# Attention's projections of chunk pairs as row tiles, with one PSUM bank per head

## The chip, the cores and the metric

The program runs on one core of one Trainium2 chip. Its time is the device time of one execution in microseconds. Before the change it is 2106.98 us, the median of three runs (2106.40 to 2107.38). The profile is of one more execution, taken by the hardware profiler.

## The reference

The program is a chain of three parts in float32: a linear attention with random features, a mixture of eight experts with balanced gates, and a feed-forward layer. The change touches the first one, for 4 batches, 8 heads, 576 tokens, a head size D of 64 and M = 128 features:

```
def phi(x):                       # x: q or k, scaled by D**-0.25
    proj = einsum('bhsd,md->bhsm', x, omega)
    sq = sum(x * x, -1) / 2
    h = proj - sq
    return exp(h - max(h, -1)) / sqrt(m)
q_p, k_p = phi(q_s), phi(k_s)
kv = einsum('bhsm,bhsd->bhmd', k_p, v)
z = sum(k_p, 2)
num = einsum('bhsm,bhmd->bhsd', q_p, kv)
den = einsum('bhsm,bhm->bhs', q_p, z) + 1e-6
out = num / den
```

## The kernel before, in words

Attention takes about the first 181 us of 2106. It works by units: one unit is a pair of heads of one batch, so there are 16, numbered from 0. The 576 tokens of a unit stand in five chunks (CH), chunk 0 of 128 tokens and chunks 1 to 4 of 112. The two heads of a pair lie in the upper and lower 64 partitions of qk, which holds the transposed and scaled q (index 0) and k (index 1).

What is done for a unit, by the names that the trace shows:

- tr: the transposes of q and k into qk's banks (qkT, L412), which ScalarE scales into qk (L421, L429).
- pr: the projection of a chunk (feat, L432), two products for q and k against bd, the block-diagonal omega: 128 rows of contraction, of which each head's features use 64 and meet zeros in the other 64. Both heads of q and k fill one PSUM bank, 4 x 128 columns.
- mx, nm, nb: VectorE's maximum over the features from that bank (L448), and two small subtractions with the squared norms sq (L450, L452).
- eq, ek: ScalarE's four exponentials of a chunk (exps, L454), which read the bank, with nb as bias; k's come first.
- kv: the sums of features and values over the five chunks, by head; zr and kz are VectorE's scaled copies of them (L484, L490).
- z, jk, den: transposed sums of features, and VectorE's row sums with eq (zT, L496). GpSimd then scales eq by the reciprocal.
- qt: transposes of eq (qpT, L532), copied to qp by ScalarE; nd: the numerators (num, L549), two 64-column tiles of TensorE's array, copied out by ScalarE (xo) and written to DRAM.

A float32 product shows as two records of TensorE in the trace, and a transpose as one.

The order is written out by hand, in rounds: the loop at L622 goes over units i and rounds r = 0 to 4, and PLAN (L612) lists each round's TensorE work and the unit that it belongs to, as an offset. Each round begins with a flush (L373): it issues the round's projection and its reduction, then everything that earlier work had put into later (ScalarE's copies and exponentials) and laterv (VectorE's, by a number), with nm and nb in between. So a chunk's exponentials are issued in the round after its projection. Chunk r is projected in round r. Each engine takes its instructions in the order in which they are issued.

Seven PSUM banks serve all of tr, pr, kv, qt and nd; an eighth is z's. A new name takes a bank that was given up, and its first product waits for the last reader of what was there. The program's own semaphore counts tell which reader that is.

Between the rounds stand steps that prepare the next phase: wprep, the weights (L639, after round 4), and xprep (L641), by XSTEPS after rounds 1 and 3 of units 8 to 15: loads, a ScalarE copy of 128x768 (L259), VectorE subtractions.

Of the kernel before, what the change touches and what calls it, by code (L numbers as in the profile page):

```python
# [9 lines left out]
F32 = mybir.dt.float32  # L10
# [9 lines left out]
def performer_moe_kernel(ctx, tc, q, k, v, omega, wg, w1, w2, win64, wout64, out):  # L20
    nc = tc.nc
# [274 lines left out]
    with ExitStack() as actx, tc.manual_schedule():  # L296
        pp = actx.enter_context(tc.tile_pool(name="pp", bufs=7, space=PSUM))

        def bank(name):
            return pp.tile([P, 512], F32, tag="b", name=name)  # L300
# [70 lines left out]
        later, laterv = [], []  # L371

        def flush(ft=iter(())):  # L373

            todo, todov = list(later), sorted(laterv, key=lambda x: x[0])
            later[:], laterv[:] = [], []
# [55 lines left out]
        def feat(u, c):  # L432

            qk, sq = T["qk", u], T["sq", u]
            o, n = CH[c]
# [5 lines left out]
            mx = a2.tile([P, 4], F32, tag="mx", name=f"mx{u}_{c}", bufs=4)  # L441
            nm = a2.tile([P, 4], F32, tag="nm", name=f"nm{u}_{c}", bufs=4)
            nb = a2.tile([P, 4], F32, tag="nb", name=f"nb{u}_{c}", bufs=4)
            ps4 = ps.rearrange("p (i m) -> p i m", i=4)
            eq = a2.tile([P, 2, M], F32, tag="eq", name=f"eq{u}_{c}", bufs=16)
            ek = a2.tile([P, 2, M], F32, tag="ek", name=f"ek{u}_{c}", bufs=7)
            T["eq", u, c], T["ek", u, c] = eq, ek
            nc.vector.tensor_reduce(mx[:n], ps4[:n], AX.X, ALU.max)  # L448
            yield
            nc.vector.tensor_tensor(nm[:n], sq[:n, c], mx[:n], ALU.subtract)  # L450
            yield
            nc.vector.tensor_tensor(nb[:n], nm[:n], sq[:n, c], ALU.subtract)  # L452

            def exps():  # L454
                for i in (2, 3, 0, 1):
                    dst = (eq, ek)[i // 2][:n, i % 2]
                    nc.scalar.activation(dst, ps4[:n, i], AF.Exp, bias=nb[:n, i : i + 1])

            T["tail feat"] = ps4, eq, ek, nb
            later.insert(0, exps)  # L460
            yield
# [137 lines left out]
        flush(feat(0, 0))  # L599
# [11 lines left out]
        NORM, RED, SPL = (0, 1), (2, 4), 4  # L611
        PLAN = [  # L612
# [625 lines left out]
```

## Time and profile before

| | |
|---|---|
| median of three runs | 2106.98 us |
| the profiled execution | 2107.69 us |
| its span | 2105.9 us |
| TensorE busy in the span | 2091.3 us |
| VectorE | 1784.4 us |
| GpSimd | 1448.0 us |
| ScalarE | 1060.7 us |
| mean granted TensorE clock | 0.999 of full speed |

The span is what the profile shows from the first to the last instruction; the profiled execution took 1.8 us more. Busy times are of the whole span, most of which is the two later parts. What attention waits for is read from its own stretch, 52 to 94 us for its steady middle.

### The profile page before, as it was taken

To read this page: it belongs to the slowest core of one execution; us is meant where nothing else is said; L and a number is where in the kernel's file an instruction comes from. 1 tells how busy PE (TensorE), PEld (TensorE's weight loads), DVE (VectorE), ACT (ScalarE), POOL (GpSimd) and SP (SyncE) were. 2 spreads that over 40 slices of the span, in tenths; PEclk is the share of its full clock that TensorE was granted. 3 is DMA by queue.
4 is the path that set the end of the run, shared out by engine and by line. 5 is a ranking of instruction groups with operands and counts; after the bars stand their busy time and mean duration, and the time that the engine had idled before them with its cause. 6 is when DMAs were issued, how large, how long until landed. Compare 5 with 4: busy or idle time off the path is not lost.

```text
span 2105.9 us, 33965 instructions
## 1 busy us (share of the span) xinstructions
PE 2091.3 (99%) x10814; PEld 1863.8 (89%) x10814; DVE 1784.4 (85%) x3468; ACT 1060.7 (50%) x2576; POOL 1448.0 (69%) x1976
## 2 busy tenths in 40 slices
PE   9999999999999999999999999999999999999999
PEld 7776898999999999989999989999999998999998
DVE  8896777889888788899888788788885689999997
ACT  6885333333334433333333433433334378888885
POOL 6776777777777777777776876777766655666652
PEclk9999999999999999999999999999999999999999
DMA  6444223232232333232232232322322231231310
GB/s 158 131 113 159 81 70 107 80 103 91 83 103 76 106 103 113 78 101 83 90 104 83 92 109 83 118 91 84 102 73 75 76 103 62 82 111 55 110 42 35
DMA packets 184371, 195.75 MB, mean 93 GB/s; under 512 B 53376, under 2 KB 142976, under 8 KB 184192
## 3 DMA queue, kind: packets, MB, share of 16 engines
q1 hardware_dynamic: 176464, 183.91, 27.7%
q10 hardware_dynamic: 7728, 9.69, 1.3%
q8 instruction: 85, 1.39, 0.3%
q14 instruction: 94, 0.77, 0.1%
HBM read 171.00 MB, written 22.54 MB: 92 GB/s over the span
## 4 chain that ended last, share of the span: by engine, by line
PE 92%; DVE 5%; ACT 1%; POOL 1%; issue 0%; DMA 0%; ACTq 0%; SPq 0%; DVEq 0%; POOLq 0%
PE l L1032 46%; PE b L925 14%; PE e L925 9%; PE a L925 9%; PE p L997 9%; PE pr L438 2%; PE kv L470 1%; DVE mx L448 1%; PE qt L389 1%; PE nd L554 1%; DVE jk L511 0%; DVE acc L1067 0%; PE tr L389 0%; DVE sq L405 0%; DVE nb L452 0%
## 5 line engine op out<-in xcount | busy, mean ns | idle before, releaser
L1032 PE MATMUL l<-v,h 128*128 128x512 f32 x4320 | 1031.1, 392 | 0.9 <-DVE second L1059 0.6
L1032 PEld LDWEIGHTS l<-v,h 128*128 128x128 f32 x4320 | 805.4, 188 | 162.9 <-DVE h L939 1.7
L86 POOL TENSOR_TENSOR v<-rs,v 128x256 fp32r<-128x256 f32 x432 | 335.1, 806 | 182.0 <-ACT v L83 172.1
L1067 DVE SCALAR_TENSOR_TENSOR acc<-l,pt,acc 128x512 f32<-128x512 f32 x516 | 375.8, 743 | 78.1 <-PE l L1032 75.7
L86 POOL TENSOR_TENSOR u<-s,u 128x256 fp32r<-128x256 f32 x384 | 293.1, 783 | 105.8 <-ACT u L83 105.4
L925 PE MATMUL b<-x,u 128*128 128x384 f32 x1728 | 351.4, 338 | 0.4 <-DVE t L952 0.4
L83 ACT CAST u<-s 128x256 fp32r<-128x256 f32 x384 | 147.0, 408 | 396.4 <-PE b L925 331.3
L925 PEld LDWEIGHTS b<-x,u 128*128 128x128 f32 x1728 | 308.5, 188 | 15.4 <-DVE t L952 0.7
L86 POOL TENSOR_TENSOR u<-rq,u 128x256 fp32r<-128x256 f32 x288 | 225.7, 784 | 128.2 <-ACT u L83 94.9
L925 PE MATMUL a<-x,u 128*128 128x384 f32 x1152 | 231.9, 335 | 1.3 <-POOL u L86 1.3
L925 PE MATMUL e<-x,u 128*128 128x384 f32 x1152 | 231.3, 335 | 0.0
L83 ACT CAST v<-rs 128x512 fp32r<-128x512 f32 x240 | 147.2, 620 | 161.2 <-PE l L1032 155.5
L997 PE MATMUL p<-x,u 128*128 128x384 f32 x1152 | 209.8, 336 | 1.1 <-DVE th L1009 1.1
L997 PEld LDWEIGHTS p<-x,u 128*128 128x128 f32 x1152 | 202.0, 188 | 5.1 <-DVE th L1009 1.5
L925 PEld LDWEIGHTS a<-x,u 128*128 128x128 f32 x1152 | 202.7, 188 | 2.7 <-POOL u L86 1.7
L925 PEld LDWEIGHTS e<-x,u 128*128 128x128 f32 x1152 | 202.8, 188 | 0.0
L1021 POOL TENSOR_TENSOR h<-t,h 128x384 fp32r<-128x384 f32 x96 | 99.0, 1031 | 131.8 <-ACT h L1020 123.6
L936 ACT ACTIVATE h<-b 128x384 fp32r<-128x384 f32 x96 | 47.3, 492 | 169.9 <-DVE b L974 169.1
L83 ACT CAST u<-rq 128x256 fp32r<-128x256 f32 x288 | 116.9, 406 | 0.8 <-ACT xo L1083 0.8
L86 POOL TENSOR_TENSOR u<-rqi,u 128x256 fp32r<-128x256 f32 x96 | 85.5, 915 | 34.4 <-ACT u L83 32.8
L936 ACT ACTIVATE h<-t 128x384 fp32r<-128x384 f32 x96 | 50.4, 525 | 115.1 <-DVE t L961 115.1
L939 DVE SCALAR_TENSOR_TENSOR h<-e,h 128x384 fp32r<-128x384 f32 x96 | 53.6, 558 | 56.3 <-ACT h L936 56.3
(176 smaller groups left out, 3046.5 us busy)
## 6 DMA issues: line engine op xcount, KB each, us to landing
rq<-in_moe_w_dram SPq DMA_DIRECT2D x96, 512.0 KB, 3.8
rs<-in_moe_w_dram SPq DMA_DIRECT2D x192, 256.0 KB, 3.1
rqi<-win SPq DMA_DIRECT2D x24, 512.0 KB, 4.4
rs<-wout SPq DMA_DIRECT2D x48, 256.0 KB, 2.8
xt<-xd SPq DMA_DIRECT2D x24, 384.0 KB, 5.4
r<-in_moe_w_in_dram SPq DMA_DIRECT2D x32, 256.0 KB, 3.0
r<-in_moe_w_out_dram SPq DMA_DIRECT2D x32, 256.0 KB, 3.1
xd<-xo SPq DMA_DIRECT2D x32, 144.0 KB, 1.8
```

Source lines behind the costliest of these rows:

```text
L83: nc.scalar.copy(dst[:, 0], src)
L86: eng.tensor_tensor(dst[:, 1, i : i + w], src[:, i : i + w], dst[:, 0, i : i + w].bitcast(F32), ALU.subtract)
L389: nc.tensor.transpose(ps[:, o - base : o - base + n], src(c, n), ident[:n, :n])
L438: nc.tensor.matmul(ps[:n, 2 * M * i : 2 * M * (i + 1)], qk[:, i, o : o + n], bd, start=True, stop=True)
L448: nc.vector.tensor_reduce(mx[:n], ps4[:n], AX.X, ALU.max)
L925: nc.tensor.matmul(ps[:, :TB], u[:, wi, c], x[:, xi, c], start=(start and m == 0), stop=(stop and m == 5), skip_group_check=True,)
L936: nc.scalar.activation(h[:, 0], src, AF.Relu)
L939: nc.vector.scalar_tensor_tensor(h[:, 1], src, 0.0, h[:, 0].bitcast(F32), ALU.max, ALU.subtract)
L997: nc.tensor.matmul(ps, u1[f + i][:, wi, c], ux[state["x0"] + 2 * t + i][:, xi, c], start=(m == 0), stop=(m == 11))
L1021: nc.gpsimd.tensor_tensor(lo, s, hi.bitcast(F32), ALU.subtract)
L1032: nc.tensor.matmul(ps, hh[f][:, hi, t : t + P], u2[n + f][:, wi], start=(f == 0 and i == 0), stop=(f == len(hh) - 1 and i == 2),)
L1067: V.scalar_tensor_tensor(a, ps, p[:, e : e + 1], a, ALU.mult, ALU.add)
```

## The change

Chunks 1 and 2 are projected together in round 1, and chunks 3 and 4 in round 3; chunk 0 stays as it was, in round 0. A pair of chunks has a bank for each head. Each product contracts over the 64 rows of one head, from its half of the partitions, into that head's bank: tile_position (64 h, 0) puts it into one half of the array's rows, and products of the two halves alternate. There are eight products of 128 columns per pair and head where there were four of 256 in all. VectorE reduces the two banks one after the other, and nm and nb are computed for the pair at once. The exponentials of a pair's first chunk are issued a round later as before; those of the second stand in the new list following, and are issued two rounds later, which is the round in which they were issued before. The preparing steps of XSTEPS stand after rounds 2 and 4 in place of 1 and 3, and the code of the last unit's ending is adapted.

```diff
@@ -368,12 +368,13 @@
-        later, laterv = [], []
+        later, laterv, following = [], [], []
...
-            later[:], laterv[:] = [], []
+            later[:], laterv[:] = list(following), []
+            following.clear()
             next(ft, None)
@@ -429,35 +430,65 @@
+        def exp1(ps, nb, u, c, i, h):
+            n = CH[c][1]
+            dst = T["eq" if i == 0 else "ek", u, c]
+            nc.scalar.activation(dst[:n, h], ps[h][:n, i], AF.Exp, bias=nb[:n, 2 * i + h : 2 * i + h + 1])
+
+        def exps(*args):
+            for i in (1, 0):
+                for h in range(2):
+                    exp1(*args, i, h)
+
-        def feat(u, c):
+        def feat(u, cs):
...
-            ps = bank(f"pr{u}_{c}")
-            for i in range(2):
-                nc.tensor.matmul(
-                    ps[:n, 2 * M * i : 2 * M * (i + 1)], qk[:, i, o : o + n], bd, start=True, stop=True
-                )
...
+            if k == 1:
+                ps = bank(f"pr{u}_{cs[0]}")
...
+            else:
+                pair = [bank(f"pr{u}_{cs[0]}_{h}") for h in range(2)]
+                for j, c in enumerate(cs):
+                    o = CH[c][0]
+                    for i in range(2):
+                        for h in range(2):
+                            m = 2 * j + i
+                            nc.tensor.matmul(
+                                pair[h][:n, M * m : M * (m + 1)],
+                                qk[D * h : D * (h + 1), i, o : o + n],
+                                bd[D * h : D * (h + 1), M * h : M * (h + 1)],
+                                start=True,
+                                stop=True,
+                                tile_position=(D * h, 0),
+                            )
+                to = mx.rearrange("p c (i h) -> p h c i", h=2)
+                pair = [t.rearrange("p (c i m) -> p c i m", c=2, i=2) for t in pair]
+                for h in range(2):
+                    nc.vector.tensor_reduce(to[:, h], pair[h][:n], AX.X, ALU.max)
+                ps = [[pair[h][:, j] for h in range(2)] for j in range(2)]
+            s = sq[:n, cs[0] : cs[0] + k]
+            yield
+            nc.vector.tensor_tensor(nm, s, mx, ALU.subtract)
+            yield
+            nc.vector.tensor_tensor(nb, nm, s, ALU.subtract)
+            todo = [lambda j=j, c=c: exps(ps[j], nb[:, j], u, c) for j, c in enumerate(cs)]
+            T["tail feat"] = ps[-1], nb[:, k - 1]
+            later.insert(0, todo[0])
+            following.extend(todo[1:])
             yield
@@ -609,6 +640,7 @@
+        FEATS = {0: [0], 1: [1, 2], 3: [3, 4]}
@@ -616,16 +648,16 @@
-        XSTEPS = {i: (1, 3) for i in range(2 * NP + 1, NUN - 1)}
-        XSTEPS[2 * NP] = XSTEPS[2 * NP + 4] = (3,)
-        XSTEPS[NUN - 1] = (1,)
+        XSTEPS = {i: (2, 4) for i in range(2 * NP + 1, NUN - 1)}
+        XSTEPS[2 * NP] = XSTEPS[2 * NP + 4] = (4,)
+        XSTEPS[NUN - 1] = (2,)
...
-                flush(feat(i, r) if i or r else iter(()))
+                flush(feat(i, FEATS[r]) if r in FEATS and (i or r) else iter(()))
```

TensorE in unit 4, rounds 3 and 4, before: pr of chunk 3, nd of round 3, qt of round 3, pr of chunk 4, nd of round 4. The number behind a name's prefix is the unit, and the words in brackets are the engines waited for.

```order
L438 MATMUL pr4_3_945<-bd_97,qk4_672 112x256 [waits DVE_49,Activation_49]
L438 MATMUL pr4_3_945<-bd_97,qk4_672 112x256
L554 MATMUL nd1_0_964<-qp1_777,kz1_106 64x288 [waits PE_49,Activation_49]
L554 MATMUL nd1_0_964<-qp1_777,kz1_106 64x288
L389 MATMUL qt2_0_968<-ident_79,eq2_0_459 128x128 [waits DVE_49,Activation_49,Pool_49]
L389 MATMUL qt2_0_968<-ident_79,eq2_1_506 128x112 [waits Pool_49]
L389 MATMUL qt2_0_968<-ident_79,eq2_2_544 128x112 [waits Pool_49]
L389 MATMUL qt2_0_968<-ident_79,eq2_3_573 128x112 [waits Pool_49]
L438 MATMUL pr4_4_975<-bd_97,qk4_672 112x256 [waits Activation_49]
L438 MATMUL pr4_4_975<-bd_97,qk4_672 112x256
L554 MATMUL nd1_1_996<-qp1_777,kz1_106 64x288 [waits DVE_49,Activation_49]
L554 MATMUL nd1_1_996<-qp1_777,kz1_106 64x288
```

The same place now, from the last records of pair (3, 4):

```order
L470 MATMUL pr4_3_0_943<-bd_97,qk4_666 112x128
L470 MATMUL pr4_3_1_944<-bd_97,qk4_666 112x128
L470 MATMUL pr4_3_0_943<-bd_97,qk4_666 112x128
L470 MATMUL pr4_3_1_944<-bd_97,qk4_666 112x128
L585 MATMUL nd1_0_965<-qp1_780,kz1_106 64x288 [waits Activation_49]
L585 MATMUL nd1_0_965<-qp1_780,kz1_106 64x288
L390 MATMUL qt2_0_969<-ident_79,eq2_0_449 128x128 [waits DVE_49,Activation_49,Pool_49]
L390 MATMUL qt2_0_969<-ident_79,eq2_1_496 128x112 [waits Pool_49]
L390 MATMUL qt2_0_969<-ident_79,eq2_2_498 128x112 [waits Pool_49]
L390 MATMUL qt2_0_969<-ident_79,eq2_3_562 128x112 [waits Pool_49]
L585 MATMUL nd1_1_986<-qp1_780,kz1_106 64x288 [waits DVE_49,Activation_49]
L585 MATMUL nd1_1_986<-qp1_780,kz1_106 64x288
```

No projection stands between qt and nd any more. By the semaphore counts, qt's first row waited for chunk 1's exponentials in its own unit before, and now for chunk 2's third one (the last reader of the pair's first bank); nd of round 4 waited for all four of chunk 2, and waits now for the fourth. The second row of a pair (1, 2), pr_1_1, waits for the third exponential of chunk 4 in the unit before, and kv of round 1 for the fourth.

VectorE in unit 4, rounds 0 and 1, before: nm and nb of chunk 0, the reduction of chunk 1, four row sums jk (each with the row that reads its sum into den) and their reciprocal; nm and nb of chunk 1 are the next rows.

```order
L450 TENSOR_TENSOR nm4_0_828<-sq4_630,mx4_0_827 128x4
L452 TENSOR_TENSOR nb4_0_829<-nm4_0_828,sq4_630 128x4
L448 TENSOR_REDUCE mx4_1_880<-pr4_1_877 112x4
L511 ISA jk2_3_0_892,den0_108<-eq2_3_573,z2_809 112x128
L511 ISA den0_108 112x1
L511 ISA jk2_3_1_894,den0_108<-eq2_3_573,z2_809 112x128
L511 ISA den0_108 112x1
L511 ISA jk2_4_0_896,den0_108<-eq2_4_600,z2_809 112x128
L511 ISA den0_108 112x1
L511 ISA jk2_4_1_898,den0_108<-eq2_4_600,z2_809 112x128
L511 ISA den0_108 112x1
L521 RECIPROCAL den0_108<-den0_108 128x4
```

The same place now, from nm of chunk 0:

```order
L485 TENSOR_TENSOR nm4_0_819<-sq4_624,mx4_0_818 128x4
L487 TENSOR_TENSOR nb4_0_820<-nm4_0_819,sq4_624 128x4
L481 TENSOR_REDUCE mx4_1_873<-pr4_1_0_876 112x4
L481 TENSOR_REDUCE mx4_1_873<-pr4_1_1_877 112x4
L542 ISA jk2_3_0_894,den0_108<-eq2_3_562,z2_801 112x128
L542 ISA den0_108 112x1
L542 ISA jk2_3_1_896,den0_108<-eq2_3_562,z2_801 112x128
L542 ISA den0_108 112x1
L542 ISA jk2_4_0_898,den0_108<-eq2_4_564,z2_801 112x128
L542 ISA den0_108 112x1
L542 ISA jk2_4_1_900,den0_108<-eq2_4_564,z2_801 112x128
L542 ISA den0_108 112x1
```

A second reduction stands ahead of the row sums. They are followed by the reciprocal, nm and nb as before, but these are now of both chunks (112x8), and those of chunk 2 are gone from the round after.

ScalarE in unit 13, rounds 1 to 3, before: the copy of xprep (CAST x), the exponentials of chunk 1, the scaling of tr, the exponentials of chunk 2.

```order
L429 ACTIVATE qk14_2612<-qt10_2_2609 128x2x112
L259 CAST x1_2666<-xt2_2530 128x768
L457 ACTIVATE ek13_1_2634<-pr13_1_2627,nb13_1_2632 112x128 x2
L457 ACTIVATE eq13_1_2633<-pr13_1_2627,nb13_1_2632 112x128 x2
L421 ACTIVATE qk14_2612<-tr14_0_2661 128x464
L457 ACTIVATE ek13_2_2675<-pr13_2_2668,nb13_2_2673 112x128 x2
L457 ACTIVATE eq13_2_2674<-pr13_2_2668,nb13_2_2673 112x128 x2
L421 ACTIVATE qk14_2612<-tr14_1_2692 128x464
```

The same place now, from the scaling of tr:

```order
L422 ACTIVATE qk14_2586<-tr14_0_2645 128x464
L259 CAST x1_2668<-xt2_2539 128x768
L436 ACTIVATE ek13_2_2604<-pr13_1_0_2608,nb13_1_2607 112x128
L436 ACTIVATE ek13_2_2604<-pr13_1_1_2609,nb13_1_2607 112x128
L436 ACTIVATE eq13_2_2603<-pr13_1_0_2608,nb13_1_2607 112x128
L436 ACTIVATE eq13_2_2603<-pr13_1_1_2609,nb13_1_2607 112x128
L422 ACTIVATE qk14_2586<-tr14_1_2663 128x464
L436 ACTIVATE ek13_3_2671<-pr13_3_0_2677,nb13_3_2676 112x128
L436 ACTIVATE ek13_3_2671<-pr13_3_1_2678,nb13_3_2676 112x128
```

The copy stood ahead of chunk 1's exponentials and stands now between the scaling of tr and chunk 2's. The exponentials alternate between the pair's two banks.

## Rows read from the trace of the kernel before

**Rows 1.** Busy time by stretch: stretch, us, then each engine's busy us, clock, DMA
```profile
10.00:20.00 10.00, 8.11 (x38) 6.01 (x37) 7.43 (x19) 7.81 (x28) 6.55 (x19) 0.83 0.77 178
52.00:94.00 42.00, 41.93 (x285) 32.98 (x284) 37.23 (x169) 33.95 (x114) 31.39 (x74) 1.00 0.45 114
```

**Rows 2.** Timeline, PE, first projections of units 3 and 15: start us, us, instruction
```profile
33.73 1.04 PE L438 MATMUL pr<-bd,qk 128*128 128x256 f32 x4
...
160.73 1.04 PE L438 MATMUL pr<-bd,qk 128*128 128x256 f32 x4
```

**Rows 3.** Waits from 52 to 136 us: total us, times, longest us
```profile
PEld nd L554 <- ACT eq L457: 3.8, 9, 0.5
...
DVE xt L236 <- DMA xt<-xd: 1.1, 1, 1.1
```

**Rows 4.** Timeline, PE, unit 6
```profile
75.41 1.04 PE L438 MATMUL pr<-bd,qk 128*128 128x256 f32 x4
...
77.54 1.28 PE L470 MATMUL kv<-vn,ek 128*128 128x128 f32 x10
78.66 0.56 PE L389 MATMUL tr<-ident,qn 128*128 128x128 f32 x4
...
81.44 1.03 PE L438 MATMUL pr<-bd,qk 128*112 128x256 f32 x4
82.40 0.71 PE L554 MATMUL nd<-qp,kz 128*64 128x288 f32 x4
83.03 0.62 PE L389 MATMUL qt<-ident,eq 128*128 128x128 f32 x4
83.49 1.03 PE L438 MATMUL pr<-bd,qk 128*112 128x256 f32 x4
84.49 0.71 PE L554 MATMUL nd<-qp,kz 128*64 128x288 f32 x4
...
85.80 1.04 PE L438 MATMUL pr<-bd,qk 128*128 128x256 f32 x4
```

**Rows 5.** Groups by line, DVE, 52 to 136 us: busy us, mean ns
```profile
L452 DVE TENSOR_TENSOR nb<-nm,sq 112x4 f32<-112x4 f32 (+1 forms) x39 | 9.7, 249 | 3.1
```

**Rows 6.** Timeline, DVE, unit 6: start us, us, instruction, idle before and its releaser
```profile
76.49 0.69 DVE L448 TENSOR_REDUCE mx<-pr 128x4 f32<-128x512 f32 x1 [0.67 <-PE pr L438]
...
79.04 0.68 DVE L448 TENSOR_REDUCE mx<-pr 112x4 f32<-112x512 f32 x1
79.64 0.27 DVE L511 CUSTOM_DVE_ANT_0 jk<-eq,z 112x128 f32<-112x128 f32 x1
...
83.12 0.68 DVE L448 TENSOR_REDUCE mx<-pr 112x4 f32<-112x512 f32 x1
```

**Rows 7.** Timeline, ACT, unit 6, and a copy of unit 10
```profile
81.29 0.63 ACT L457 ACTIVATE ek<-pr,nb 112x128 f32<-112x128 f32 x2 [0.44 <-PE kv L470]
...
82.30 0.57 ACT L421 ACTIVATE qk<-tr 128x464 f32<-128x464 f32 x1
83.29 0.63 ACT L457 ACTIVATE ek<-pr,nb 112x128 f32<-112x128 f32 x2 [0.41 <-DVE nb L452]
83.81 0.63 ACT L457 ACTIVATE eq<-pr,nb 112x128 f32<-112x128 f32 x2
84.31 0.57 ACT L421 ACTIVATE qk<-tr 128x464 f32<-128x464 f32 x1
84.74 0.65 ACT L457 ACTIVATE ek<-pr,nb 112x128 f32<-112x128 f32 x2
...
85.75 0.46 ACT L566 COPY xo<-nd 128x288 f32<-128x288 f32 x1
...
86.77 0.46 ACT L457 ACTIVATE ek<-pr,nb 112x128 f32<-112x128 f32 x1
...
112.21 0.87 ACT L259 CAST x<-xt 128x768 fp32r<-128x768 f32 x1
112.93 0.67 ACT L457 ACTIVATE ek<-pr,nb 112x128 f32<-112x128 f32 x2
```

More of the change, by code (lines that the diff above doesn't have):

```diff
@@ new lines, in exps @@
+        def exps(*args):
[3 more added lines that the diff above has]
+        def feat(u, cs):
+            qk, sq = T["qk", u], T["sq", u]
+            n, k = CH[cs[0]][1], len(cs)
+            for c in cs:
+                T["eq", u, c] = a2.tile([P, 2, M], F32, tag="eq", name=f"eq{u}_{c}", bufs=16)
+                T["ek", u, c] = a2.tile([P, 2, M], F32, tag="ek", name=f"ek{u}_{c}", bufs=7)
+            mx, nm, nb = (
+                a2.tile([P, 2, 4], F32, tag=t, name=f"{t}{u}_{cs[0]}", bufs=4)[:n, :k] for t in ("mx", "nm", "nb")
+            )
+            if k == 1:
+                ps = bank(f"pr{u}_{cs[0]}")
+                o = CH[cs[0]][0]
+                for i in range(2):
+                    nc.tensor.matmul(
+                        ps[:n, 2 * M * i : 2 * M * (i + 1)], qk[:, i, o : o + n], bd, start=True, stop=True
+                    )
+                nc.vector.tensor_reduce(mx[:, 0], ps[:n].rearrange("p (i m) -> p i m", i=4), AX.X, ALU.max)
+                ps4 = ps.rearrange("p (i h m) -> p h i m", i=2, h=2)
+                ps = [[ps4[:, h] for h in range(2)]]
+            else:
+                pair = [bank(f"pr{u}_{cs[0]}_{h}") for h in range(2)]
+                for j, c in enumerate(cs):
+                    o = CH[c][0]
+                    for i in range(2):
+                        for h in range(2):
+                            m = 2 * j + i
+                            nc.tensor.matmul(
+                                pair[h][:n, M * m : M * (m + 1)],
[4 more added lines that the diff above has]
+                                tile_position=(D * h, 0),
+                            )
+                to = mx.rearrange("p c (i h) -> p h c i", h=2)
[4 more added lines that the diff above has]
+            s = sq[:n, cs[0] : cs[0] + k]
@@ L449, in feat @@
             yield
-            nc.vector.tensor_tensor(nm[:n], sq[:n, c], mx[:n], ALU.subtract)
+            nc.vector.tensor_tensor(nm, s, mx, ALU.subtract)
             yield
[L452 to L459, printed above, removed]
@@ L460, in feat @@
-            later.insert(0, exps)
+            nc.vector.tensor_tensor(nb, nm, s, ALU.subtract)
[3 more added lines that the diff above has]
+            following.extend(todo[1:])
             yield
@@ L598, in performer_moe_kernel @@
         nc.scalar.mul(qk0[:, :, :P], ps0[:, : 2 * P].rearrange("p (i n) -> p i n", i=2), SC)
-        flush(feat(0, 0))
+        flush(feat(0, [0]))
         squares(range(1, NCH))
@@ L656, in performer_moe_kernel, with last_exps @@
         y, z = NUN - 2, NUN - 1
-        ps4, eq, ek, nb = T["tail feat"]
-        n = CH[-1][1]
-        def exps(i):
+        tail = *T["tail feat"], z, NCH - 1
+        def last_exps(i):
             for h in range(2):
-                j = 2 * i + h
-                nc.scalar.activation((eq, ek)[i][:n, h], ps4[:n, j], AF.Exp, bias=nb[:n, j : j + 1])
+                exp1(*tail, i, h)
         later.pop(0)
-        exps(1)
+        last_exps(1)
         qpT(y - 1, 2)
@@ L669, in performer_moe_kernel @@
         now(later[1:])
-        exps(0)
+        last_exps(0)
         now(later[:1])
```

9 lines of the change are left out of this document (removed).

## Prediction

> **What bounds the kernel now.** I read the busy times by stretch first. From 52 to 94 us, in the middle of attention, TensorE is busy 41.93 of 42 us at full granted clock, VectorE 37.23 and ScalarE 33.95 [rows 1]: TensorE ends last, and the two others are close behind. The reader is to see there that a cheaper TensorE cannot win more than the gap to VectorE, 4.7 us in 42, and not even that if a wait comes up. Next I read TensorE's timeline for the length of a unit (one pair of heads; there are 16): units 3 and 15 open with their first projection at 33.73 and 160.73 us, so the 12 units between take 10.58 us each [rows 2]. One of them holds a wait of VectorE for a transfer, 1.1 us [rows 3]. Unit 6 takes 10.39 us, from 75.41 to 85.80 [rows 4]. Last I read the waits: TensorE's loads for nd wait 9 times for chunk 2's exponentials, 3.8 us in 52 to 136 us, and most of the rest is other engines waiting for something [rows 3]. So one loop across engines is already about as long as TensorE's work. Everything after attention (from about 181 us) is untouched and shifts as a block.
>
> **What the change removes from TensorE.** A unit has five projections; four of them become two pairs. An unpaired one lasts from 81.44 to the next product's start at 82.40, less 0.10 for that product's change to tiles: 0.86 us, so 1.72 for two [rows 4]. A pair has 8 products of 128 columns for each half, and each product is two records in the trace: 16 records. kv's ten records of 128 columns last 1.12 us (77.54 to 78.66), 0.112 each [rows 4]. No row has row tiles. Below: if both halves run together, as the two column halves of nd do, 8 x 0.112 = 0.90; above: one after the other, 1.79. What tiles cost in turning the array comes from nd: its four records of 288 columns last 0.63 (82.40 to 83.03), two by two they need 2 x 288/128 x 0.112 = 0.50, so 0.13, and 0.10 ahead of it [rows 4]. A pair costs 1.13 or 2.02 us. I take 1.13, since nd is the nearest row: 0.59 saved per pair, 1.2 per unit, and TensorE's work falls from 10.4 to 9.2 us. Above, it grows by 0.3 per pair.
>
> **What it does to VectorE and ScalarE.** Reductions stay five of the same size. Of the five pairs of nm and nb three stay: four instructions less, nb lasting 0.25 us and nm about as long [rows 5], at most 1.0 us of VectorE's work per unit. The twenty exponentials stay, with the same shapes. So busy times all fall or stay. The cost is in the waits.
>
> **The wait that takes over.** A pair's two banks hold both chunks, so they come free only when the second chunk's exponentials, one round later, have read them. In the order shown, qt of round 3 took a bank that chunk 1 had left a round earlier; now it takes the first bank of pair (1, 2), and so waits for the third exponential of chunk 2; nd of round 4 takes the second bank and waits for the fourth. Behind qt on TensorE stand nd, z, qt and the next unit's first projection, and for that wait VectorE's reduction, and all of VectorE's chain to the next chunk 2. This closes a loop of one turn per unit:
> - TensorE, from qt to VectorE's first reduction: qt 0.46 (83.03 to 83.49), the change to tiles 0.10, nd, z and qt 1.31 (84.49 to 85.80) [rows 4], first projection to its reduction 1.08 (75.41 [rows 4] to 76.49 [rows 6]): 2.95.
> - VectorE, first reduction to the second one: 2.55 (76.49 to 79.04), with six row sums, nm and nb between and no gap to shorten [rows 6].
> - From there to chunk 1's exponentials 2.25 (79.04 [rows 6] to 81.29 [rows 7]); now two reductions stand there, and one more takes 0.60 (79.04 to 79.64) [rows 6]: 2.85.
> - ScalarE: chunk 1's four exponentials 1.01 (81.29 to 82.30), the scaling of tr 0.43 (84.31 to 84.74), chunk 2's first two 0.52 (83.29 to 83.81), the third 0.38 (the two of 83.81 last 0.63 and start 0.25 apart), and 0.05 to TensorE's start (84.44 to 84.49, [rows 4, 7]): 2.39.
>
> Sum 10.74 us, against 10.58 now with its transfer wait and about 10.5 without. TensorE's saving becomes idle time ahead of qt. In before the same chain had chunk 2's own reduction after chunk 1's, and closed at a nd that stood behind one more projection; it was a little under 10.4, hence the nine short waits.
>
> **The copies that move.** Steps that prepare the next phase now stand after rounds 2 and 4 in place of 1 and 3. Four of these steps in units 9 to 14 hold a ScalarE copy of 0.72 us (112.21 to 112.93) [rows 7]. It stood ahead of chunk 1's exponentials, where ScalarE was waiting for VectorE anyway; now it stands between the scaling and chunk 2's exponentials, inside the loop. 4 x 0.72 = 2.9 us. Bounds: nothing if ScalarE's loop has slack there, 0.87 each (the copy's own length) at most. VectorE's subtractions now stand after round 4, ahead of the reduction that waits for TensorE; VectorE's work of 8.2 to 9.2 us a unit leaves it 1.5 to 2.5 idle in a loop of 10.74, so they cost nothing; without that idle time, up to about the copy's length each. The transfer's wait of 1.1 us stays [rows 3]; SP's queue has the same order around it but for one row.
>
> **Sum.** 12 x 10.74 + 2.9 + 1.1 = 132.9 us for units 3 to 14, against 127.0 (160.73 - 33.73): 5.9 us longer. The first units have no full loop, and the last one's ending has the same exponentials last: nothing for both, half a microsecond either way. The profiled execution took 2107.69 us (span 2105.9), so 2113.6 on its scale; it lies 0.7 above the median of the runs, 2106.98. Forecast: 2113 us. The loop's own bounds: 10.5 if the change to tiles and the hand-over to TensorE overlap, 11.0 if the second loop (below) mixes in: 2109 to 2118.
>
> The Trainium skill speaks against the change here, on the page TensorEngine Tiling (Array Packing), section Restrictions and Gotchas: row tiling raises the pressure on PSUM, because row tiles write to different banks. The waits of [rows 3] agree that banks are short already. That page, under Performance Considerations, gives packed tiles up to a full factor of two; by that alone the sum would be TensorE's 9.2 us a unit, which is the first rival.
>
> **Rivals.**
> 1. TensorE's saving is kept, because no bank wait comes last. For it: TensorE busy 41.93 of 42 [rows 1]; a loop under 10.4 us would be hidden, and mine is 3% above that, so the point from which it decides is an error of 0.35 us in a sum of ten terms. Against it: every term was measured with its engine dense. The unit would be bounded by VectorE, 37.23/42 of 10.4 = 9.2: 12 x (9.2 - 10.58) = -16.6, so 2090 us; with half of it 2099. Chance 0.18.
> 2. The halves don't run together. Then a second loop decides: the second pair's exponentials, chunk 4's third one, the next unit's first pair (its second bank is the one that chunk 4 leaves), and on to the second pair. Pair 2.02, kv and tr twice 2 x (1.12 + 0.46), pair 2.02 [rows 4], about 0.2 to the reduction, 1.62 + 0.60 to chunk 3's exponentials (83.12 [rows 6] to 84.74 [rows 7]), four of them 1.01, copies 1.02 (85.75 to 86.77), three of chunk 4 0.90, 0.05 [rows 7]: 12.6 at most, some 0.4 less where no weight copy stands. With 12.2: 12 x (12.2 - 10.58) = +19.4, so 2126 us. With 1.13 for a pair the same loop is 10.8 at most, beside the forecast's 10.74. Chance 0.15.
> 3. TensorE's clock falls. Between 10 and 20 us, where TensorE was busy 8.1 of 10, the granted clock was 0.83 on average, so part of it was at 1.2 GHz [rows 1]. The forecast leaves TensorE idle for about 1.5 us ahead of qt in each unit. If what follows ran at 1.2 in place of 2.4 GHz, TensorE's 2.95 us of the loop would grow by about 2.5 us: 12 x 2.5 = 30 on top, 2143 us. Against it: the clock is 1.00 in all later attention though waits of 0.5 us are there. Chance 0.08.
>
> **How the numbers follow.** Forecast 0.59, 2109 to 2118; rivals 0.18, 0.15, 0.08. Eight in ten: 2101 to 2130, which takes in the forecast, rival 2 and the half of rival 1. A difference under 0.2%, here 4.2 us, cannot be told from none: of the forecast about a third lies under 2111.2, 0.21, and of rival 1 0.03. Faster 0.15, same 0.24, slower 0.61.
>
> **What would show it.** A unit of 10.6 to 10.9 us between first projections, and 11.4 where the copy stands; TensorE's busy time in 52 to 94 us down to about 36, with the gap ahead of qt and the releaser chunk 2's exponential; the pair's records starting two by two, 1.1 us a pair; VectorE's busy time down by nearly 4 us in that stretch. I am wrong if the gap ahead of qt is missing, if the pair lasts 2 us, or if the clock row shows under 1.00 there.

## The result, and the profile after

The changed kernel takes 2121.13 us (median of four runs, 2117.66 to 2122.84); the kernel before took 2106.99 us beside it. The ratio is 1.0062, 95% interval [1.0050, 1.0075]: slower by 13 us. The profiled execution after took 2120.79 us, span 2119.0.

All of it lies in attention. The first projection of unit 3 starts at 34.80 us (33.73 before, [rows 2]), that of unit 15 at 174.09 (160.73), so units 3 to 14 take 139.29 us where they took 127.00. What follows unit 15 is 0.3 us shorter.

Busy time by stretch after (us, then PE, PEld, DVE, ACT, POOL, the granted clock, DMA), beside [rows 1]:

```profile
10.00:20.00 10.00, 7.60 (x49) 5.98 (x50) 7.34 (x18) 6.85 (x25) 6.40 (x19) 0.67 0.76 176
...
52.00:94.00 42.00, 36.81 (x334) 29.49 (x330) 32.76 (x148) 33.17 (x113) 30.88 (x73) 1.00 0.46 116
94.00:136.00 42.00, 34.51 (x288) 26.64 (x286) 32.73 (x130) 30.73 (x102) 26.90 (x61) 0.92 0.46 122
136.00:168.00 32.00, 28.17 (x229) 22.93 (x228) 24.16 (x104) 22.92 (x77) 21.11 (x47) 0.89 0.38 103
```

TensorE has lost 5 us of work in 42, and nobody else has become busier: the time is a wait. From 94 us on the granted clock is no longer 1.00. TensorE's timeline, unit 7 and one later row, beside [rows 4]. (The rows that are headed unit 6 before the prediction, and called so in it, are unit 7's too: counted from unit 3 at 33.73 us, the projection at 75.41 is the fifth one. The sums don't hang on the name.)

```profile
75.58 0.59 PE L390 MATMUL qt<-ident,eq 128*128 128x128 f32 x4
...
77.41 1.04 PE L457 MATMUL pr<-bd,qk 128*128 128x256 f32 x4
...
78.77 1.16 PE L470 MATMUL pr<-bd,qk 64*112 64x128 f32 x16
...
83.10 1.13 PE L470 MATMUL pr<-bd,qk 64*112 64x128 f32 x16
85.42 0.71 PE L585 MATMUL nd<-qp,kz 128*64 128x288 f32 x4 [1.18 <-ACT qk L422]
86.24 0.59 PE L390 MATMUL qt<-ident,eq 128*128 128x128 f32 x4
...
113.06 1.94 PE L457 MATMUL pr<-bd,qk 128*128 128x256 f32 x4
```

A pair's 16 records last 1.13 to 1.16 us here, so the two halves do run together. (In the first pairs of units 8, 9, 11 and 12 they last 1.46 us; that time is hidden, since VectorE reaches their reduction later still.) Behind the second pair TensorE stands still for 1.18 us in every plain unit, until ScalarE has scaled the transposes whose bank nd takes. The last row is a first projection at half the clock: 1.94 in place of 1.04 us. The waits of 52 to 136 us (total, times, longest) show that gap as the largest of TensorE's, where [rows 3] had 3.8 us:

```profile
ACT ek L436 <- DVE nb L487: 21.2, 15, 3.4
...
PEld nd L585 <- ACT qk L422: 12.2, 9, 1.8
```

The chain of waits from 77 to 89 us shows the loop itself (start, us, what), one turn from z to z:

```profile
76.81 0.37 PE z L532 x2
77.18 0.40 PE qt L390 x4
77.58 0.89 PE pr L457 x4
78.49 0.69 DVE mx L460
79.18 0.20 DVE jk L542
...
80.46 0.19 DVE den L552
80.65 0.05 DVE nm L485
80.75 0.04 issue
80.80 0.16 DVE nb L487
80.96 1.20 DVE mx L481 x2
82.16 0.19 DVE jk L542
...
83.02 0.18 DVE den L552
83.19 0.14 DVE nm L485
83.43 0.26 DVE nb L487
83.73 0.05 issue
83.77 0.16 ACT ek L436
...
84.40 0.52 ACT eq L436 x2
84.92 0.46 ACT qk L422
85.42 0.71 PE nd L585 x4
86.12 0.12 issue
86.24 0.59 PE qt L390 x4
86.83 0.64 PE nd L585 x4
87.46 0.37 PE z L532 x2
```

The reader is to see that the chain passes TensorE, VectorE and ScalarE once each and comes back to the same place 10.65 us later (87.46 less 76.81). TensorE is on it for 3.7 us, from nd to the reduction's start in the next unit, and has 5.6 us of other work beside it; of VectorE everything between the two reductions and behind them is on it, the row sums jk too, which nobody on this path needs.

Units 3 to 7 take 10.65 us each; units 8 to 14 take 11.37, 13.62, 12.28, 11.39, 12.60, 12.49 and 12.27. Three things lengthen them. The first is ScalarE's copy, in units 9, 10, 13 and 14. ScalarE's timeline shows it between the scaling and chunk 2's exponentials; their distance is 0.44 us in unit 7 and 1.16 in unit 9:

```profile
84.79 0.57 ACT L422 ACTIVATE qk<-tr 128x464 f32<-128x464 f32 x1
85.23 0.65 ACT L436 ACTIVATE ek<-pr,nb 112x128 f32<-112x128 f32 x2
...
107.53 0.57 ACT L422 ACTIVATE qk<-tr 128x464 f32<-128x464 f32 x1
107.97 0.86 ACT L259 CAST x<-xt 128x768 fp32r<-128x768 f32 x1
108.69 0.66 ACT L436 ACTIVATE ek<-pr,nb 112x128 f32<-112x128 f32 x2
```

The second is VectorE's two subtractions, in units 8, 9, 11 and 12. Chunk 0's do the same as in unit 7 and last two to three times as long; in VectorE's timeline, unit 7 (with the second reduction behind them) and then unit 9:

```profile
80.57 0.12 DVE L485 TENSOR_TENSOR nm<-sq,mx 128x4 f32<-128x4 f32 x1
80.80 0.16 DVE L487 TENSOR_TENSOR nb<-nm,sq 128x4 f32<-128x4 f32 x1
80.88 1.28 DVE L481 TENSOR_REDUCE mx<-pr 112x4 f32<-112x512 f32 x2
...
102.59 0.31 DVE L485 TENSOR_TENSOR nm<-sq,mx 128x4 f32<-128x4 f32 x1
103.01 0.47 DVE L487 TENSOR_TENSOR nb<-nm,sq 128x4 f32<-128x4 f32 x1
```

In unit 9 GpSimd is at work when both start; in unit 7 it idles from 80.03 to 80.83 us, so that neither meets it at its start. From unit 8 on a weight step (L86, 0.73 us) goes ahead of GpSimd's squares; in units 10, 13 and 14 the slow clock puts VectorE's subtractions behind them all the same.

The third is TensorE's clock, which stood at 1.2 GHz (granted clock 0.50) in three stretches: 109.1 to 115.9 us, 146.6 to 150.0, 160.3 to 163.7.

Summed by segments of the loop, units 3 to 14 are 12 x 10.65 = 127.8, copies 4 x 0.74 = 3.0, longer subtractions 4 x 0.72 = 2.9, and TensorE's segments at half clock, against the same ones of unit 7, 1.5, 0.9, 1.2, 1.1 and 0.9 in units 9, 10 and 12 to 14, 5.6: 139.3.

### The profile page after: what moved, and what is told of

The parts are those of the page before. It is cut to its first block, busy times and chain, and to the rows that moved or that the text cites. A ratio compares the mean times of both kernels' runs of the same rounds, so it can differ in the third digit from the quotient of the medians.

```text
span 2119.0 us, 34344 instructions
## 1 busy us (share of the span) xinstructions
PE 2083.3 (98%) x11070; PEld 1860.7 (88%) x11070; DVE 1773.1 (84%) x3404; ACT 1058.3 (50%) x2576; POOL 1452.7 (69%) x1976
## 4 chain that ended last, share of the span: by engine, by line
PE 91%; DVE 5%; ACT 2%; issue 1%; POOL 1%; DMA 0%; SPq 0%; ACTq 0%; DVEq 0%; POOLq 0%
PE l L1062 45%; PE b L955 14%; PE e L955 9%; PE a L955 9%; PE p L1027 9%; DVE jk L542 1%; PE nd L585 1%; PE pr L457 1%; DVE mx L481 1%; PE qt L390 1%; DVE acc L1097 0%; DVE mx L460 0%; ACT ek L436 0%; ACT eq L436 0%; PE pr L470 0%
## 5 line engine op out<-in xcount | busy, mean ns | idle before, releaser
L86 POOL TENSOR_TENSOR v<-rs,v 128x256 fp32r<-128x256 f32 x432 | 335.5, 807 | 181.1 <-ACT v L83 171.3
L86 POOL TENSOR_TENSOR u<-s,u 128x256 fp32r<-128x256 f32 x384 | 293.0, 782 | 110.3 <-ACT u L83 110.0
L86 POOL TENSOR_TENSOR u<-rq,u 128x256 fp32r<-128x256 f32 x288 | 226.1, 785 | 132.3 <-ACT u L83 99.9
L86 POOL TENSOR_TENSOR u<-rqi,u 128x256 fp32r<-128x256 f32 x96 | 85.6, 916 | 34.0 <-ACT u L83 32.7
```

The lines of the kernel that those rows point to most:

```text
L86: eng.tensor_tensor(dst[:, 1, i : i + w], src[:, i : i + w], dst[:, 0, i : i + w].bitcast(F32), ALU.subtract)
```

## The experiments

All ratios are to the kernel before, run on the same chip; "a plain unit" is one of units 3 to 7.

**The copies back in rounds 1 and 3.**

```diff
-        XSTEPS = {i: (2, 4) for i in range(2 * NP + 1, NUN - 1)}
+        XSTEPS = {i: (1, 3) for i in range(2 * NP + 1, NUN - 1)}
```

> The preparing steps go back behind rounds 1 and 3; all else is the changed kernel (2121.1 us). Theory (a loop over TensorE, VectorE and ScalarE, 10.65 us a unit, closed by the pairs' banks): the four copies of 0.72 us leave the loop, units 9, 10, 13 and 14 get shorter by 0.7 each, 2.9 in all: about 2118 us, with ScalarE's span from chunk 1's to chunk 2's exponentials 1.45 in every unit (2.17 in those four before). Rival (the late units are long because the granted clock falls, and the copies are hidden): 2121 us, the late units as long as they were.

2116.17 us, ratio 1.0046 [1.0029, 1.0062]: 5.0 us less. From chunk 1's exponentials to chunk 2's it is 1.45 us in every unit, units 9, 10, 13 and 14 included: the four copies were 3.0 us of the loop. The rest, by which the time lies about 2 us under my 2118, is the clock, which fell less often here (units 3 to 14: 134.2 us, 12 x 10.65 + 2.9 for the subtractions leaves 3.5). A plain unit is still 10.65.

**Pairs without row tiles.** The same banks, order and pairs, each product over all 128 rows with the zeros.

```diff
-                                qk[D * h : D * (h + 1), i, o : o + n],
-                                bd[D * h : D * (h + 1), M * h : M * (h + 1)],
+                                qk[:, i, o : o + n],
+                                bd[:, M * h : M * (h + 1)],
...
-                                tile_position=(D * h, 0),
```

> The pairs keep their banks and their order, but each product runs over all 128 rows of the array, against the half of the block-diagonal omega that has the zeros: no row tiles. Theory: a pair lasts 16 x 0.107 = 1.7 us in place of 1.13, so the second loop (pair (3, 4), its exponentials, the bank of the next pair (1, 2)) grows from about 10.4 by 2 x 0.6 to 11.6 us a unit: 12 x 1.0 = 12 us more, less some 4 of the clock that falls less often: about 2129 us. Rival (row tiles bring nothing, since TensorE idles ahead of nd anyway): 2117 to 2121 us, a unit of 10.65.

2118.20 us, ratio 1.0054 [1.0039, 1.0069]. Two pairs of one unit in TensorE's timeline:

```profile
81.80 1.78 PE L470 MATMUL pr<-bd,qk 128*112 128x128 f32 x14 [0.31 <-ACT eq L436]
...
86.47 1.91 PE L470 MATMUL pr<-bd,qk 128*112 128x128 f32 x16
```

A pair lasts 1.91 against 1.13 us, and a unit 11.24 us from unit 5 on (10.64 and 11.00 in units 3 and 4; theory 11.6, after 10.65): the tiles do what they say and are worth 0.6 us a unit. The wait ahead of nd is gone. Instead VectorE waits 1.34 us for the second pair, ScalarE 1.03 us for its biases, and the next first pair 0.31 us for chunk 4's exponentials: this is the second loop, which the forecast priced under rival 2, and it sets the 11.24 us.

The time, however, is that of the rival, 2.9 us under the changed kernel's. The clock stays at 1.00 from 20 us on, which is worth 5.6 us, and units 8 to 14 take 81.5 us, only 2.8 more than seven of 11.24, where copies and subtractions cost 5.9 in the changed kernel. I had 12 us for the units and 4 off for the clock: the direction of both was right, and the growth of the units much too large, since units 3 to 7 are only 2.1 us longer in all and the later ones, clock left out, 1.1.

**The gap filled.** Four products that nobody reads, into an unused part of z's bank, ahead of nd in round 3.

```diff
+            for _ in range(4 if s == 0 and u < NUN - 3 else 0):
+                nc.tensor.matmul(T["zt"][:, 2 * M : 3 * M], ones, ones, start=True, stop=True)
```

> Four products of ones into a free part of z's bank stand ahead of nd of round 3 in each unit, about 0.9 us of TensorE in a gap of 1.2 to 1.9 us; their values are read by nothing. Theory (three falls of the granted clock cost 5.6 us in the profiled execution, and they come from the gap): the clock stays at 1.00 from 25 us on, plain units stay at 10.65, and the time is 2115 to 2118 us with little spread. Rival (the falls have nothing to do with the gap): 2121 us and clock rows under 1.00 as before.

2116.07 us, ratio 1.0042 [1.0027, 1.0057]: more work on TensorE and 5.1 us less time. A plain unit is 10.69, no shorter. What is gone shows in the clock of the two later stretches, 0.92 and 0.89 in the changed kernel:

```profile
94.00:136.00 42.00, 38.82 (x340) 31.12 (x338) 33.96 (x138) 33.23 (x112) 28.64 (x64) 1.00 0.54 143
136.00:168.00 32.00, 29.12 (x264) 24.11 (x264) 28.03 (x117) 24.20 (x80) 23.68 (x54) 1.00 0.31 80
```

So the falls cost 5 us, and they come from TensorE's standing still in the loop.

**The row sums out of the loop.** In round 0 VectorE does the sums (jk) first and chunk 0's reduction behind them.

```diff
-            for _ in range(3):
+            for _ in range(4):
...
+                if u > 1:
+                    yield
                 nc.vector.tensor_reduce(mx[:, 0], ps[:n].rearrange("p (i m) -> p i m", i=4), AX.X, ALU.max)
```

> VectorE's six row sums of round 0 are issued ahead of chunk 0's reduction, in the time in which VectorE waits for the projection (2.07 us in each unit). Nothing else moves. Theory: the first loop gets shorter by 1.36 us (six sums and a reciprocal), from 10.65 to 9.3 us; the second loop of about 10.4 us then decides: plain units 10.4, the four with a copy and the ones with slow small VectorE instructions 10.4 to 10.8 in place of 11.4 to 12.3: about 2114 to 2118 us. Rival (TensorE's waits ahead of nd come from ScalarE's load alone, and VectorE's order is of no account): 2121 us, 10.65 a unit.

2112.54 us, ratio 1.0026 [1.0016, 1.0035], 1.5 us under my range. Units 6 to 8 take 9.92, 10.19 and 10.47 us, where I had 10.4 for the second loop, so that one is shorter than I took it for. No instruction was taken away, only moved off the chain, and the unit is up to 0.7 us shorter: that is the direct proof that the loop sets the unit. Two things beside it count in the time. Units 3 and 4 are longer than before the edit, 11.49 and 10.85 us, with TensorE at half clock from 35.7 to 39.2; and from 52 us on the clock stays at 1.00, so the three falls are missing too.

**The same order in the kernel before.**

```diff
+            if c == 0 and u > 1:
+                yield
             nc.vector.tensor_reduce(mx[:n], ps4[:n], AX.X, ALU.max)
```

> The kernel before with the sums of round 0 put ahead of chunk 0's reduction on VectorE, as in the run that put them first in the changed kernel; nothing is left out. My theory (before, TensorE's own work sets the unit, so VectorE's order is worth nothing there, while in the changed kernel it sits in the loop of banks): plain units stay at 10.34 to 10.40 us, a time of 2105 to 2108. Rival (that order is a gain of its own that has nothing to do with the loop): plain units fall by 0.2 us or more, a time of 2100 to 2104.

2110.56 us, ratio 1.0015 [1.0005, 1.0024]. Units 7 to 11 keep their length (10.38 at unit 7, 10.56 at unit 10; 10.39 and 10.58 before), so VectorE's order is worth nothing where TensorE sets the pace. The time is 2.6 us outside my range, on the slow side: units 2 to 5 lose 3.3 us together. In units 3 to 5 chunk 0's reduction comes 1.80 to 2.67 us behind its projection's start, in place of 1.07 to 1.21, because VectorE is still at the sums; unit 3 takes 11.58 us. That this delay is the loss is not shown: units 6 and 7 have it too, 1.80 and 1.81 us, and lose nothing.

**Both chunks' exponentials in the round after the pair.**

```diff
-            later.insert(0, todo[0])
-            following.extend(todo[1:])
+            if k == 2 and not (u == NUN - 1 and cs[0] == 3):
+                later[0:0] = todo
+            else:
+                later.insert(0, todo[0])
+                following.extend(todo[1:])
```

> The changed kernel with the exponentials of both chunks of a pair put into the round behind the pair, so that both banks of the pair come free a round earlier; nothing is left out. My theory (the loop is set by who needs which bank next, not by how long a bank is held): qt of round 3 no longer waits for chunk 2's third exponential, but the banks now pass on in another order: nd of round 3 takes the bank that chunk 2's third exponential frees and qt the fourth's, so the loop keeps both exponentials and nd's 0.5 us enters it while the scaling's half microsecond leaves: a plain unit of 10.8 to 11.2 us, a time of 2119 to 2126. Rival (the second chunk's late exponentials alone hold the loop; freeing them early ends it): a plain unit of 9.9 to 10.3 us and a time of 2110 to 2115.

2118.38 us, ratio 1.0056 [1.0041, 1.0071], and a plain unit of 10.81 to 10.82 us, as the theory had it (its time lies 0.6 us under the theory's range): the rival's 9.9 to 10.3 is out. A bank that is given up earlier helps nobody if the next name to take it is one that needs it as early; nd now waits for the exponential that qt waited for:

```profile
76.04 0.71 PE L588 MATMUL nd<-qp,kz 128*64 128x288 f32 x4 [1.52 <-ACT eq L436]
```

**The biases straight behind the pair's reductions**, copies in rounds 1 and 3, and in the first of two runs the sums first as well.

```diff
-            yield
+            if k == 1:
+                yield
             nc.vector.tensor_tensor(nm, s, mx, ALU.subtract)
-            yield
+            if k == 1:
+                yield
             nc.vector.tensor_tensor(nb, nm, s, ALU.subtract)
```

> The changed kernel with three edits of order, all on VectorE and ScalarE: the sums of round 0 ahead of chunk 0's reduction, the two subtractions that make a pair's biases directly behind the pair's reductions (the sums and kz behind them), the early copies in rounds 1 and 3; nothing is left out. My theory (the loop of banks runs from the reductions over the biases to the exponentials): what stands between the reductions and the exponentials leaves the loop, which falls to about 8.2 us; the next limit is the loop through the pair of chunks 3 and 4, 9.4 to 9.9 us; plain units of 9.4 to 10.1 us, a time of 2097 to 2107. Rival (TensorE's clock falls more when its gaps move, or TensorE's own 9.3 us come first with a wait I have not seen): plain units of 10.2 us or more, a time of 2110 or more.

> The changed kernel with two edits of order: the two subtractions that make a pair's biases stand directly behind the pair's reductions on VectorE, and the early copies stand in rounds 1 and 3; the sums of round 0 stay where the change has them. Nothing is left out. My theory (the loop of banks sets the unit; in the run with three edits the sums put first made chunk 0's reduction late instead): the step from the pair's reductions to the exponentials falls from 2.90 to 2.0 us, the loop to about 9.8 us; VectorE, busy 9.5 us a unit and more where GpSimd runs beside its short instructions, is as near: plain units of 9.8 to 10.4 us, a time of 2101 to 2108. Rival (VectorE is the limit by now and the order changes nothing): plain units of 10.2 to 10.5 us and 2108 to 2112.

With the sums first 2109.89 us, ratio 1.0012 [1.0003, 1.0022]; without that edit 2111.48, ratio 1.0019 [1.0011, 1.0028]. They miss their ranges by 2.9 and 3.5 us, and the second one's rival has its time. Units 4 and 5 are as forecast, 10.03 us in the first run and 10.1 in the second. Units 6 to 11 are longer, 10.2 to 10.6. The run with the sums first shows why, in the busy times of its middle:

```profile
52.00:94.00 42.00, 39.77 (x356) 32.05 (x355) 38.72 (x154) 34.73 (x118) 31.37 (x74) 1.00 0.45 117
```

VectorE is busy 38.72 of 42 us, and in units 6 to 11 its timeline has no idle time: the loop has given way to a full engine. Part of that fullness is waiting inside an instruction. From its VectorE's timeline, and GpSimd's of the same moment:

```profile
93.26 1.20 DVE L488 TENSOR_TENSOR nm<-sq,mx 112x8 f32<-112x8 f32 x1
94.56 0.25 DVE L491 TENSOR_TENSOR nb<-nm,sq 112x8 f32<-112x8 f32 x1
```

```profile
92.68 1.75 POOL L559 TENSOR_TENSOR eq<-eq,den 128x256 f32<-128x256 f32 x3
```

The same nm, for the other pair, lasted 0.17 us at 66.78 of this run.

In the run without that edit VectorE is not full: in units 4 to 9 it stands idle 0.89 us a unit ahead of chunk 0's reduction. TensorE's z waits there for VectorE's copy zr (52 to 136 us):

```profile
PEld z L534 <- DVE zr L517: 4.5, 8, 0.6
```

Its chain of waits closes at that place, from z at 78.04 to z at 88.49 us: TensorE's z, qt and first projection, and then VectorE's whole order from chunk 0's reduction to zr, 8.64 us. So a third loop sets 10.4 us there, with most of VectorE's work in it.

The two runs also start later than the kernel before (unit 3 at 36.94 and 37.07 us, before 33.73), with TensorE at half clock for 13 and 10 us before 40 us, where the kernel before has 3.4.

**Chunk 4's exponentials directly behind chunk 3's**, on the run with the sums first.

```diff
+            if cs[0] == 3 and u < NUN - 1:
+                later[0:0] = todo
+            else:
```

> The run with the three edits of order, and chunk 4's exponentials directly behind chunk 3's, except in the last unit; nothing is left out. My theory (the loop through the pair of chunks 3 and 4 is the next limit, and holds its second bank until chunk 4's exponentials a round later): plain units 0.1 to 0.4 us below those of the run with the three edits alone, 2 to 5 us off its time. Rival (another wait or TensorE's work is the limit by then): no difference over 1 us.

2112.86 us, ratio 1.0028 [1.0017, 1.0040]: 3.0 us more, which neither theory expected. Units 4 and 5 shrink by the 0.14 us that the loop through chunk 4 held (9.89). In units 10 and 11 nb lasts 1.10 and 1.11 us and the unit 11.05: the shift moved VectorE's short instructions under GpSimd's long ones. In units 8 to 11 nm and nb last 0.43 to 0.46 us a unit longer than in the run before, and the units are 0.41 to 0.47 longer.

**Without the norms**: changed order, changed kernel, and kernel before. From unit 1 on GpSimd squares nothing, VectorE sums no squares, and a bias is the negated maximum.

```diff
-                if r in NORM and i + 1 < NUN:
+                if False:
...
+            if u == 0:
                 nc.vector.tensor_tensor(nm, s, mx, ALU.subtract)
+            else:
+                nc.vector.tensor_scalar(nb, mx, -1.0, None, ALU.mult)
```

> The changed kernel without the norms from unit 1 on, order unchanged (the norm cancels against the maximum; what is left out is its rounding). My theory (the loop of banks sets the unit, so only what stands in the loop counts): the two subtractions that fall out of the loop take 0.5 to 0.6 us off it, the other 2 us of VectorE's work that go are not in it: plain units of 10.0 to 10.2 us, the units 8 to 12 no longer stretched, a time of 2108 to 2114. Rival (VectorE's total work is the limit): plain units of 9.5 us or less, a time of 2104 or less.

> The kernel before without the norms from unit 1 on, in the same way as in the run on the changed kernel (the norm cancels against the maximum; what is left out is its rounding). My theory (TensorE's own work sets the unit there, so freeing VectorE and GpSimd is worth little): plain units of 10.3 to 10.4 us to the end, the later ones 0.1 to 0.2 us shorter than with the norms, a time of 2103 to 2106. Rival (VectorE is the limit already before): plain units below 10.1 us, a time under 2102.

> The run with the two edits of order, without the norms from unit 1 on: GpSimd squares nothing, VectorE sums no squares, and a bias is the negated maximum in one instruction (the norm cancels against the maximum; what is left out is its rounding). My theory (row tiles take 1 us or more a unit off TensorE, and what ate it is first the loop of banks and then VectorE, which was busy 9.2 to 9.5 of every 10.4 us; with both relieved it must show): plain units of 9.3 to 9.8 us, a time of 2092 to 2100, 7 us or more below the kernel before without its norms. Rival (the row tiles gain nothing that could be had; another limit stands at 10.3 us): plain units of 10.2 us or more, within 3 us of the kernel before without its norms.

The changed kernel takes 2106.11 us, ratio 0.9992 [0.9983, 1.0001], 15.0 us less than with the norms and 1.9 below my range. A plain unit is 10.02 us: 0.63 less, the two subtractions in the loop, though VectorE has lost three times that (32.76 of 42 us busy before the edit, 27.06 behind it: 8.3 and 6.5 us a unit). So the loop, not VectorE's total, sets the changed kernel's unit, and the rival's 9.5 is out. Units 8 and 11 are 10.03 and 10.05, not stretched: with GpSimd's squares gone the one instruction that makes the biases lasts 143 ns on average. The clock is 1.00 from 52 us on. 12 x 0.63 + 2.9 + 5.6 = 16.1; less 0.6 for a later start and 1.6 for unit 12, which takes 11.60 because VectorE waits 2.2 us for a transfer in it, this is 13.9, as between the two profiled executions (2120.79 and 2106.87).

The kernel before takes 2103.87 us, ratio 0.9981 [0.9972, 0.9990]. In its middle TensorE has no gap at all, and of units 3 to 14 all but unit 12 (10.51) are 10.34 or 10.35 us; that is TensorE's work with whole projections:

```profile
52.00:94.00 42.00, 42.00 (x286) 33.26 (x285) 30.14 (x140) 34.31 (x116) 15.42 (x26) 1.00 0.51 133
```

The run with the two edits of order takes 2102.96 us, ratio 0.9977 [0.9968, 0.9987]; the same stretch:

```profile
52.00:94.00 42.00, 40.35 (x364) 32.02 (x360) 30.07 (x134) 35.60 (x119) 16.38 (x27) 1.00 0.49 124
```

Here the theory loses, and of the rival only the time holds. Its units are 9.58 to 10.26 us, but for 11.22 in unit 12, and all of units 3 to 14 take 121.4 us against 124.3, so something of the row tiles can be had, but 3 us and not 7; and the start eats it: unit 3 begins at 35.94 us against 31.39, with TensorE at half clock from 15 to 22 us, where the kernel before without norms shows 1.00 throughout. In the middle new small gaps stand, z's for VectorE's copy zr the largest (5.9 us in 52 to 136), and a wait of the first pair for chunk 4's exponentials:

```profile
64.87 0.44 PE L538 MATMUL z<-ident,zr 128*128 128x128 f32 x2 [0.59 <-DVE zr L521]
```

```profile
PEld pr L470 <- ACT eq L436: 1.8, 5, 0.4
```

The chain of waits shows what they belong to. In unit 5, 10.26 us, it closes from z to z over TensorE's work up to the second pair and VectorE's reductions, nb and zr. From unit 10 to unit 11, 10.14 us, it closes at the first pair. VectorE waits 1.68 us for the second pair, ScalarE 0.37 for its biases, and the first pair 0.17 for chunk 4's exponentials: the second loop again. With the first loop out of the way, others of nearly its length stand behind it.

The run with the two edits beats the kernel before and the changed one, but by the norms: the kernel before without them is as fast within both intervals. No version that keeps the norms beat the kernel before.

## Why the prediction was right or wrong

Forecast 2113 us, range 2101 to 2130, slower; measured 2121.13. The way and the range are right; the size is not: 14.1 us more than before where the forecast had 6, and outside the 2109 to 2118 that it gave as the loop's own bounds. The loop itself was right; what it left out, the clock and the longer subtractions, is 8.5 us.

- **Right: the loop takes over.** Forecast 2.95 + 2.55 + 2.85 + 2.39 = 10.74 us a unit, measured in unit 7 2.91 + 2.39 + 2.89 + 2.47 = 10.66, from qt (75.58) to the first reduction (78.49), to the second (80.88), to the exponentials (83.77), and back to qt (86.24). The sums put first and the norms left out show the cause: what is taken off the chain shortens the unit, what is taken off elsewhere does not.
- **Nearly right: where the gap stands.** I put it ahead of qt, released by chunk 2's third exponential. It stands one instruction earlier, ahead of nd, released by the scaling of tr; qt follows nd directly. Both paths end within 0.1 us of each other, which is why the sum held; that closeness was in no step of the forecast and is luck. In the units with the copy qt starts 1.55 us after nd in place of 0.82: there, by the semaphore counts, it is the exponential; the profile names no releaser for that wait.
- **Right: the pair.** 1.13 forecast, 1.13 to 1.16 measured in a plain unit; TensorE's work 36.81 of 42 us, 9.3 a unit, against 9.2. Rival 2, halves one after the other, is out. Its second loop exists, but was priced too long: 12.2 us with pairs of 2.02, measured 11.24 with pairs of 1.91. The forecast's 9.2 us beside the factor of two is its own sum with 1.13 us a pair; a full factor would leave 10.4 - 1.72 = 8.7, and the pair measured 1.13 against 1.72.
- **Right: the copies**, 2.9 forecast, 3.0 measured.
- **Wrong by 1.1, harmless: the wait for a transfer.** I kept it on the path; it lies now in VectorE's wait for chunk 0's projection (0.92 us, up to 136.64, and the projection starts at 136.73).
- **Mis-sized: TensorE's clock.** The forecast had nothing for it; rival 3 had 30 us, for every unit. It fell in three stretches, 5.6 us by segments, 5.1 by the run with the gap filled. The argument against it, that waits of 0.5 us had left the clock alone, says nothing on gaps of 1.2 to 1.6. The sign that was named for it, a clock under 1.00 from 52 to 94 us, did not show: the falls come later.
- **Mis-sized: nm and nb.** I had nb at the mean of [rows 5], 249 ns, without asking why a mean was above the shortest, and the loop's steps hold nm and nb as one unit shows them. They are in the loop now and take 2.9 us more in four units.
- **Unclear: the start.** I gave nothing either way; unit 3 starts 1.07 us later, with TensorE at half clock for 6.8 us there in place of 3.4 (0.67 against 0.83 in [rows 1]). The run with the copies put back has the same code up to unit 8 and starts unit 3 at 35.61, 0.8 later still, so a start is known to about a microsecond. Every run on the changed kernel starts unit 3 later than the kernel before does, 34.80 to 37.11 us, and 35.44 and 35.94 against 31.39 without the norms; no run tells why.

On the profiles' scale: 2113.6 - 1.1 (loop) - 1.1 (transfer) + 2.9 + 5.6 + 1.1 (start) - 0.3 (end) + 0.1 (copies) = 2120.8.

Where TensorE's saving went, then: the 1 us a unit is turned into a wait; behind that wait stand other limits of nearly its length, in one run VectorE, which [rows 1] had at 37.23 of 42 and which has no idle time left there, in another a loop with most of VectorE's work in it; and TensorE's idle time comes back as a lower clock.

## What to carry to other kernels

When a change makes a bank serve two pieces of work, write down who takes each bank next and follow that chain through every engine back to its start: its length is a bound of its own, and what is moved off it is gained, while work off the chain is free. Before making the busiest engine cheaper, look at the second and third; here TensorE had 10.35 us of work a unit, the new loop took 10.65, and with that shortened VectorE or a loop through it took 10.2 to 10.6. Idle time on TensorE is not free either: the wait that it repeats here cost 5 us by its clock.

## What the runs showed of the hardware

- In units 3 to 7, with a gap of 1.18 us in each 10.65, TensorE's clock stayed at 2.4 GHz. Units 8 and 9 have gaps of 1.60 and 1.59 us, and it fell to 1.2 GHz about 1 us behind the second (nd at 108.16, clock at 109.1); units 11 and 12 have 1.62 and 1.60, and it fell 1.1 us behind the second of these (145.45, 146.6). The third fall, at 160.3, came after a gap of 1.26 in unit 13, so the gap's length alone does not tell it. Units 9 and 13 have a second wait ahead of qt, 0.84 and 0.85 us; unit 14, with 1.18 and 0.85, has no fall. With the gap filled there was none from 25 to 180 us.
- A subtraction of 112x8 numbers took 0.17 us or 1.20, with GpSimd scaling eq beside the long one, which ends at 94.46 us, 0.03 behind GpSimd's three scalings. In the changed kernel's unit 9 nm ends at 102.90 us, and so do GpSimd's squares beside it. The Trainium skill, SBUF — State Buffer, section SBUF: two separate sides, has a rule for it: VectorE and GpSimd share a pair of ports, which one of them holds for its whole instruction, and a VectorE instruction with two SBUF inputs waits for a GpSimd instruction that reads SBUF and began before it. The runs agree: nm and nb have two such inputs; the one-input bias of the runs without norms, with fewer instructions on GpSimd, lasted 143 ns on average. Fewer inputs and less of GpSimd were not tried apart, and that the long one outlasts about two of GpSimd's three instructions the rule alone does not say.
- TensorE stands 0.12 us between nd's column tiles and the whole-array qt (86.12 to 86.24), about the price that the forecast took from nd.
